# Gradient of four decode layers on one core: other positions for the last K and dK products of the last pass

## The chip, the cores and the metric

The kernel runs on one core of a Trainium2 chip. The metric is the device time of one execution in microseconds (us); less is better. The core's engines work side by side, each through its own instructions in order: PE (TensorE: matrix products and transposes), DVE (VectorE), ACT (ScalarE), POOL (GpSimd) and SP (SyncE). In this kernel SP issues the loads from memory (DMA queue q1), POOL the stores (q0), and ACT a few weight loads (q10); all of them are carried out by the same 16 DMA engines. PE writes to PSUM only, and DVE or ACT then copies ("evacuates") the result to on-chip memory.

## What is computed

Attention over a cache of 65,536 keys and a feed-forward layer, twice each with the same weights, for one token; and, for a given gradient of the result, the gradients with respect to the input, the caches, the weights and the biases. Cut to what matters:

```python
def A_ref(x, k_cache, v_cache, wq, wo):       # 32 query heads, 4 key/value groups, 128 wide
    q = (x @ wq) ...
    p = softmax(q @ K^T * Dh**-0.5)
    return (p @ V) @ wo
x = x + A_ref(layernorm(x), A_k_cache, A_v_cache, A_wq, A_wo)
x = x + B_ref(layernorm(x), ...)              # relu(h)^2 feed-forward
x = x + A_ref(layernorm(x), A_k_cache, A_v_cache, A_wq, A_wo)
x = x + B_ref(layernorm(x), ...)
# out_0 = x; out_1.. = vjp(grad_out): d x, d k_cache (out_2), d v_cache (out_3), d wq (out_4), d wo, ...
```

K and V caches are 64 MB each, so each is read in all four passes, and their gradients (another 64 MB each) are written in the last.

## The kernel before

The kernel goes through the caches in four passes: forward of the first attention, forward of the second, backward of the second, and the **last pass** (`attn_bwd4`), which is the backward of the first attention and writes the K and V gradients of both layers. Only the last pass is touched by the change.

**Items and half-blocks.** The last pass has 256 *items* (`ITEMS[3]`), in four groups of 64; an item is 8 columns of 128 keys. Four items make a *half-block* of 1 MB (`J` = 32 columns), the unit that is loaded (`kv8`, line 361) and stored (line 1441). I number the half-blocks of the last group from the end: V5, V4, ... V0 and K5, K4, ... K0, so that K0 is loaded and used last.

**Stages and lags.** `pipeline` (line 846) runs in steps. For each stage, item k is handled in step k + lag + 16 (the 16 is `LEAD`; the V stages run ahead by up to 16 steps at the start of the pass, by none from item 64 on). In the order of a step the stages are: `vT` transposes an item of V (lag 0; L1354 on PE, evacuated at L164 or L161 to `kt`), `vS` computes dP from it (lag 2; L1391, then X at L1412), `eIn` and `eT` prepare the saved probabilities (L1363, L1369), `dV8` forms outer products for dV (lag 3; L1435, from `GG[1]`), `xT` transposes X (lag 6; L1369), `dK8` forms outer products for dK (lag `DK_LAG` = 7; L1435, from `GG[0]`), and `k8` multiplies X with an item of K (lag `B4_LAG` = 11; L1466, eight products per item, 32 per half-block). Each half-block gives 1 MB of dV or dK: four PSUM tiles `ps_gg` of 128 x 1024, each made by two products of L1435 and cast to bf16 by ACT (L161) or DVE (L164) before the store. `ps_gg` has two buffers, shared with the other outer products (L1513, which form the weight gradients) and with the small L1498 transposes that prepare their rows.

**The end.** When the last K product is there, `fold_dq` (L1198 to L1203) forms the last group's dq, and `on4` runs the last chain: L723 multiplies dq with transposed weights, the layernorm's backward follows, and `g_outer_last` forms the last part of the gradient of wq: three preparations at L1498 (two of them, `rowa`, partly need nothing of dq), eight tiles at L1513, four stores of 512 KB at L1534. Three functions are placed by their distance from the end of the pipeline (`end`): `last_v`, which issues the loads of V2, V1 and V0 together; the weight loads `wq4` on ACT (L459); and `fill4`, which begins the transposes at L689. With a largest lag of 11 the pipeline has 283 steps and these stand in steps 260, 263 and 273.

**Where loads go.** On-chip memory has 20 slots of 1 MB (`ARENA`). In the last pass stores (`fill`) keep to one set of slots and loads to another, of seven slots. A load takes the slot that has been free longest in the program's order, and on the chip it waits until that slot's last user is done: for a slot that held K, the last L1466 product of that half-block; for one that held V, the last L1354 transpose. SP issues its loads in order, so one that waits holds up those behind it.

**Order.** Outside of `manual_schedule` blocks the order of each engine's instructions is made by a scheduler when the program is built; a step in `pipeline` decides what an instruction's place is in the program, not exactly where it comes out. The last pass is outside such blocks.

Of the kernel before, what the change touches and what calls it, by code (L numbers as in the profile page):

```python
# [20 lines left out]
def kernel(  # L21
# [44 lines left out]
    TLEAD = 2  # L66
# [213 lines left out]
    def hold(i):  # L280
        HELD.add(i)
        FREE.pop(i, None)
# [124 lines left out]
    DK_LAG = TLEAD + J // 8 + 1  # L407
    B4_LAG = DK_LAG + J // 8
    DV_LAG = TLEAD + 1
# [433 lines left out]
    def tasks(i):  # L843
        for fn in TASKS.pop(i, ()):
            fn()

    def pipeline(items, stages, bg, end=(), holds=(), lead=None):

        def due(lag):
            at = {}  # L850
            for k, it in enumerate(items):
                at.setdefault(k + lag + LEAD if lead is None or lag >= 0 else k + ~lag + lead(k), []).append(it)
            return at
        LEAD = 0 if lead is None else lead(len(items))
        when = [due(l) for _, l in stages]
        maxlag = max(l for _, l in stages) + LEAD
        for i in range(len(items) + maxlag):
            NOW["i"] = i
            NOW["wide"] = NOW["pairs"]
            for at, k in holds:  # L860
                if i == at:
                    hold(k)
            tasks(i - 0.5)
            for n, (fn, lag) in enumerate(stages):
                for it in when[n].get(i, ()):
                    fn(*it)
                if n == 0:
                    tasks(i)
            bg.step(max(0, i - LEAD))
            NOW["wide"] = False  # L870
            NOW["step"] += 1
            for before, fn in end:
                if i == len(items) + maxlag - before:
                    fn()
        while TASKS:
            k = min(TASKS)
            NOW["i"] = int(k + 0.5)
            tasks(k)
# [128 lines left out]
    def attn_fwd(p, L, on_group, bg, end=()):  # L1007
# [178 lines left out]
        with tc.manual_schedule(engines=ORDERED):  # L1186
            pipeline(items, [(kT, 0), (kS, TLEAD), (v8, FWD_LAG)], bg, end, holds)
# [19 lines left out]
    def attn_bwd3(p, L, on_group, bg, end=()):  # L1207
# [85 lines left out]
        with tc.manual_schedule(engines=ORDERED):  # L1293
            pipeline(items, [(vT, 0), (vS, TLEAD), (k8, B3_LAG)], bg, end)
# [3 lines left out]
    def attn_bwd4(p, La, Lb, on_group, bg, stack, end=()):  # L1298
        dspool = stack.enter_context(tc.tile_pool(name="b4_ds", bufs=2))
        items = ITEMS[p]  # L1300
# [181 lines left out]
        for b in range(V_LEAD * 8 // J // 2):  # L1482
            nexts.append(("k",) + items[(b + 2) * J // 8])
            nexts.append(("v",) + items[(b + NKEEP[2]) * J // 8])
        pipeline(items, [(vT, ~0), (vS, ~TLEAD), (eIn, 0), (eT, TLEAD), (dV8, DV_LAG), (xT, DK_LAG - 1), (dK8, DK_LAG), (k8, B4_LAG)], bg,
                 end, lead=V_SHIFT)


# [148 lines left out]
    bg = Background()  # L1637
# [39 lines left out]
    bg = Background()  # L1677
# [165 lines left out]
    bg = Background()  # L1843
# [130 lines left out]
    bg = Background()  # L1974
# [42 lines left out]
    def fill4():  # L2017
# [5 lines left out]
                                  lastg[3] * 1024)  # L2023
        next(PRE["gwq"])
    attn_bwd4(3, L1, L3, on4, bg, b4, [(12 + B4_LAG, last_v), (20, pre_load("wq4", lambda: wq_slabs(lastg[3], 2))), (10, fill4)])
    b4.close()
    ps4_stack.close()
# [30 lines left out]
```

## Time and profile before

| | us |
|---|---|
| three runs | 1932.66, 1934.70, 1939.24 |
| their median | 1934.70 |
| the profiled execution's own time | 1936.54 |
| its span, first to last instruction | 1934.7 |
| PE busy (matmul) | 1595.9 (82%) |
| DVE busy / ACT busy | 1171.8 (61%) / 1044.5 (54%) |
| mean rate of the DMA engines | 407 GB/s |
| last K product (L1466) starts | at 1900.30 |
| last evacuation ends, last store issued | 1928.1, 1928.36 |

The busy shares are means over four passes with different limits. What matters here is the stretch from about 1846 us to the end: what PE, the loads and the two `ps_gg` buffers do there. A row of the timeline gives the start, the busy time, the engine, the line, the operation with what it writes and reads, how many instructions of it stand together, and in brackets the engine's idle time before it with what ended it. A row of the windows gives, for a stretch of time, the busy time and number of instructions of each engine, the TensorE clock that was granted (1.00 is full), the share of the DMA engines' time and their rate.

### The profile page before, as it was taken

What the parts mean: (1) busy time and instruction counts of PE and PEld (TensorE: products, weight loads), DVE (VectorE), ACT (ScalarE), POOL (GpSimd) and SP (SyncE); (2) the same over time, 40 slices, a digit from 0 to 9 for tenths busy, and PEclk for the clock granted to TensorE, in tenths of its full rate; (3) what the DMA queues carried; (4) which work ended last, traced back from release to release, by engine and by line L of the source; (5) the groups of instructions that cost most, each with busy time, mean ns of one, the idle gap of its engine ahead of it and who ended that gap; (6) DMA issues with size and microseconds to landing.
All of it is one profiled execution on the core that took longest, in us unless ns stands there. A gap on an engine that the chain in (4) does not pass through costs nothing. (4 is left out here: it accounts for less than half of the span.)

```text
span 1934.7 us, 66770 instructions
## 1 busy us (share of the span) xinstructions
PE 1595.9 (82%) x30099; PEld 1303.7 (67%) x30099; DVE 1171.8 (61%) x2448; ACT 1044.5 (54%) x1619; POOL 143.4 (7%) x325
## 2 busy tenths in 40 slices
PE   6878788688778878978787888888978979789796
PEld 6878778678777778877777885555555555456463
DVE  5655555255555554645454576777867777667685
ACT  3434333345333545445363465666867677667676
POOL 0000000000000000000000002111211111111111
PEclk9989998799999998999899999898988889788896
DMA  9999999999999999999999997999999999999997
GB/s 394 426 428 424 427 429 416 403 420 415 428 425 428 429 414 327 376 426 429 425 426 422 404 366 285 425 424 386 424 425 423 424 402 407 393 403 416 421 419 301
DMA packets 107148, 787.62 MB, mean 407 GB/s; under 512 B 9440, under 2 KB 16622, under 8 KB 42222
## 3 DMA queue, kind: packets, MB, share of 16 engines
q1 hardware_dynamic: 78558, 609.26, 76.2%
q0 software_dynamic: 24080, 165.70, 20.5%
q10 hardware_dynamic: 4224, 8.39, 1.1%
q8 instruction: 235, 3.85, 0.7%
q14 instruction: 51, 0.42, 0.1%
HBM read 617.62 MB, written 165.69 MB: 405 GB/s over the span
## 5 line engine op out<-in xcount | busy, mean ns | idle before, releaser
L164 DVE COPY kt<-ps_tr 128x1024 bf16<-128x1024 bf16 x736 | 504.9, 688 | 434.6 <-PE ps_tr L1031 240.3
L161 ACT CAST arena<-ps_gg 128x1024 bf16<-128x1024 f32 x457 | 444.4, 1012 | 204.1 <-PE ps_gg L1435 136.3
L1031 PE MATMUL ps_tr<-ident_b,arena 128*128 128x128 bf16 x3840 | 312.4, 227 | 49.7 <-DMA arena<-in_A_k_cache_dram 37.0
L161 ACT COPY kt<-ps_tr 128x1024 bf16<-128x1024 bf16 x180 | 188.3, 1051 | 190.7 <-PE ps_tr L1225 108.9
L164 DVE CAST arena<-ps_gg 128x1024 bf16<-128x1024 f32 (+2 forms) x186 | 222.1, 1194 | 88.5 <-PE ps_gg L1435 51.1
L1031 PEld LDWEIGHTS <-arena 128*128 128x128 bf16 x3840 | 235.3, 102 | 58.6 <-DMA arena<-in_A_k_cache_dram 39.6
L1132 PE MATMUL ps_acc<-arena 128*128 128x64 bf16 (+4 forms) x4096 | 204.2, 196 | 46.4 <-DMA arena<-in_A_v_cache_dram 29.4
L1435 PE MATMUL ps_gg<-GG,xt 64*128 64x512 bf16 x1024 | 216.8, 420 | 19.5 <-ACT arena L161 8.8
L1354 PE MATMUL ps_tr<-ident_b,arena 128*128 128x128 bf16 x1824 | 181.2, 235 | 30.3 <-DMA arena<-in_A_v_cache_dram 16.4
L1049 PE MATMUL ps_sc<-L_qpad,kt 128*128 128x64 bf16 (+7 forms) x3584 | 183.5, 194 | 17.9 <-issue 10.9
L1114 ACT ACTIVATE arena<-S_sb,L_negm 128x128 bf16<-128x128 f32 x256 | 165.1, 1005 | 60.3 <-DVE L_negm L1099 60.3
L1225 PE MATMUL ps_tr<-ident_b,arena 128*128 128x128 bf16 x2032 | 161.7, 224 | 40.7 <-DMA arena<-in_A_v_cache_dram 39.0
L1132 PEld LDWEIGHTS <-arena 128*128 128x128 bf16 x4096 | 159.4, 101 | 52.4 <-DMA arena<-in_A_v_cache_dram 33.0
L1354 PEld LDWEIGHTS <-arena 128*128 128x128 bf16 x1824 | 120.7, 105 | 88.4 <-issue 68.7
L1049 PEld LDWEIGHTS <-kt 128*128 128x128 bf16 x3584 | 153.3, 100 | 21.8 <-issue 11.7
L1225 PEld LDWEIGHTS <-arena 128*128 128x128 bf16 x2032 | 122.6, 100 | 46.8 <-DMA arena<-in_A_v_cache_dram 41.3
L1466 PEld LDWEIGHTS <-arena 128*128 128x128 bf16 x2048 | 91.1, 101 | 63.1 <-DMA arena<-in_A_k_cache_dram 32.2
L1114 ACT ACTIVATION_READ_ACCUMULATOR arena<-S_sb,L_negm 128x1 f32 x256 | 128.0, 500 | 0.0
L1391 PEld LDWEIGHTS <-kt 128*128 128x128 bf16 x1824 | 85.2, 102 | 50.3 <-issue 48.7
L1391 PE MATMUL ps_sc<-DOB,kt 128*128 128x64 bf16 (+3 forms) x1824 | 118.2, 198 | 0.1
L1466 PE MATMUL ps_acc<-X,arena 128*128 128x64 bf16 (+3 forms) x1536 | 94.8, 197 | 26.3 <-DMA arena<-in_A_k_cache_dram 26.3
L585 ACT ACTIVATE mv_t<-mv_t 128x1024 bf16<-128x1024 bf16 x96 | 102.0, 1064 | 21.6 <-DVE mv_t L596 21.5
(319 smaller groups left out, 2102.8 us busy)
## 6 DMA issues: line engine op xcount, KB each, us to landing
arena<-in_A_k_cache_dram SPq DMA_DIRECT2D x82, 2048.0 KB, 21.4
arena<-in_A_v_cache_dram SPq DMA_DIRECT2D x79, 2048.0 KB, 20.7
out_dram<-arena POOLq DMA_DIRECT2D x149, 1024.0 KB, 15.2
arena<-in_A_v_cache_dram SPq DMA_DIRECT2D x84, 1024.0 KB, 12.6
arena<-in_A_k_cache_dram SPq DMA_DIRECT2D x84, 1024.0 KB, 12.8
arena<-in_A_wo_dram SPq DMA_DIRECT2D x22, 1024.0 KB, 13.9
arena<-in_B_w_dram SPq DMA_DIRECT2D x21, 1024.0 KB, 10.0
arena<-in_A_wq_dram SPq DMA_DIRECT2D x7, 2048.0 KB, 25.4
```

The lines of the kernel that those rows point to most:

```text
L161: nc.scalar.copy(out=out, in_=in_)
L164: nc.vector.tensor_copy(out=out, in_=in_)
L585: nc.scalar.activation(out=t[:, :], in_=t[:, :], func=ACTF.Copy, accum_out=y[:, kc:kc + 1])
L1031: nc.tensor.transpose(pt[:, i, :], kb8[:, i, :], ident_b[:, :])
L1049: nc.tensor.matmul(state["ps_s"][:, s:s + w, :].rearrange("p a b -> p (a b)"), lhsT=kt[:, i, :], rhs=L["qpad"][:, g, 0:w, :].rearrange("p ...
L1114: nc.scalar.activation(out=E(p, g, c0, SU)[:, :, h], in_=S[:, h, :], func=ACTF.Exp, bias=L["negm"][:, g, su, h:h + 1], scale=SCALE, accum_ ...
L1132: nc.tensor.matmul(ps_o[:, 0:w, :], lhsT=vb8[:, i, :], rhs=E(p, g, c, w), start=(c % SU == 0), stop=(c % SU == SU - 1), skip_group_check=True)
L1225: nc.tensor.transpose(pt[:, i, :], vb8[:, i, :], ident_b[:, :])
L1354: nc.tensor.transpose(pt[:, i, :], vb8[:, i, :], ident_b[:, :])
L1391: nc.tensor.matmul(state["ps_dp"][:, s:s + w, :].rearrange("p a b -> p (a b)"), lhsT=vt[:, i, :], rhs=DOB[:, g, 0:w, :].rearrange("p a b - ...
L1435: nc.tensor.matmul(pg[:, 512 * h:512 * h + 512], lhsT=xt[64 * h:64 * h + 64, j1 // 8 + m, :], rhs=gg[64 * h:64 * h + 64, :, :].rearrange(" ...
L1466: nc.tensor.matmul(ps_dq[:, 0:w, :].rearrange("p a b -> p (a b)"), lhsT=kb8[:, i, :], rhs=X[:, s:s + w, :].rearrange("p a b -> p (a b)"), ...
```

## The change

It lets the lag of a stage be a function of the item, and gives two stages such a function at the end of the pass.

- `k8`: the last 16 items (half-blocks K3 to K0) get a smaller lag. It is 11 for the sixteenth item from the end, then 10, 10, 10 for K3; 9, 9, 9, 8 for K2; 8, 8, 7, 7 for K1; 7, 6, 5, 5 for K0. The last K product moves from step 282 to step 276.
- `dK8`: the items of the second last half-block get lag 11 in place of 7, those of the last get 9. Their dK outer products move from steps 273 and 274 to 277 and 278 (second last) and from 277 and 278 to 279 and 280 (last).
- `maxlag`, from which the number of steps follows, is now 25 in place of 27, so the pipeline has 281 steps, and the three functions placed from its end move by two steps: `last_v` from 260 to 258, `wq4` from 263 to 261, `fill4` from 273 to 271.

```diff
         def due(lag):
             at = {}
+            if callable(lag):
+                for k, it in enumerate(items):
+                    at.setdefault(k + lag(k) + LEAD, []).append(it)
+                return at
             for k, it in enumerate(items):
                 at.setdefault(k + lag + LEAD if lead is None or lag >= 0 else k + ~lag + lead(k), []).append(it)
             return at
         LEAD = 0 if lead is None else lead(len(items))
         when = [due(l) for _, l in stages]
-        maxlag = max(l for _, l in stages) + LEAD
+        maxlag = max(l(len(items) - 1) if callable(l) else l for _, l in stages) + LEAD
...
-        pipeline(items, [(vT, ~0), (vS, ~TLEAD), (eIn, 0), (eT, TLEAD), (dV8, DV_LAG), (xT, DK_LAG - 1), (dK8, DK_LAG), (k8, B4_LAG)], bg,
+
+        def k_lag(k):
+            left = len(items) - 1 - k
+            return B4_LAG - min(5, (max(0, 15 - left) + 2) // 3) - (left < 2)
+
+        def dK_lag(k):
+            left = len(items) - 1 - k
+            return DK_LAG + (0 if left >= 8 else 4 if left >= 4 else 2)
+        pipeline(items, [(vT, ~0), (vS, ~TLEAD), (eIn, 0), (eT, TLEAD), (dV8, DV_LAG), (xT, DK_LAG - 1), (dK8, dK_lag), (k8, k_lag)], bg,
                  end, lead=V_SHIFT)
```

## The prediction

> **What bounds the kernel now.** First the page's slices, then stretches of the last 90 us, then the timeline where the change begins.
>
> ```profile
> span 1934.7 us, 66770 instructions
> ...
> PEclk9989998799999998999899999898988889788896
> DMA  9999999999999999999999997999999999999997
> ```
>
> DMA is full up to the last slice, the clock is not.
>
> ```profile
> 1846.00:1856.00 10.00, 9.40 (x136) 5.89 (x133) 8.13 (x19) 7.78 (x9) 2.31 (x4) 1.00 1.01 422
> ...
> 1886.00:1896.00 10.00, 9.60 (x124) 6.41 (x123) 8.29 (x13) 8.51 (x10) 1.06 (x2) 1.00 1.02 422
> ...
> 1904.00:1914.00 10.00, 8.92 (x86) 4.86 (x83) 5.28 (x16) 5.54 (x8) 1.25 (x2) 0.50 0.58 239
> 1914.00:1924.00 10.00, 6.56 (x29) 1.56 (x28) 5.88 (x7) 5.55 (x6) 2.34 (x4) 0.50 0.63 262
> ```
>
> In the first two rows PE is busy 94 and 96% at full clock, more than DVE (81 and 83%) and ACT (78 and 85%): the rows say that PE's own queue sets the pace, and what PE loses there comes late at the end. From 1904 on nothing is full: there the two `ps_gg` buffers go round (fill, cast, fill), at half clock.
>
> Where the last K product stands, and how the loads before it are timed:
>
> ```profile
> 1845.57 0.37 PE L1466 MATMUL ps_acc<-X,arena 128*128 128x64 bf16 x8
> ...
> 1845.97 0.33 SPq L361 DMA_DIRECT2D arena<-in_A_v_cache_dram  x1
> ...
> arena<-in_A_v_cache_dram SPq DMA_DIRECT2D x1, 1024.0 KB, 9.1
> ...
> 1855.92 0.31 PE L1466 MATMUL ps_acc<-X,arena 128*128 128x64 bf16 x6
> ...
> 1900.30 0.18 PE L1466 MATMUL ps_acc<-X,arena 128*128 128x16 bf16 x1
> ```
>
> K7's last products start at 1845.57 and free a slot; V0's load goes out 0.2 us after their end, and lands 9.1 us later, at 1855.1. K6's last six start at 1855.92, K0's last at 1900.30.
>
> **The change, part by part.** *K's smaller lags.* Nothing is added or removed; products move in PE's queue. The order of the built program shows how far: K3's last product comes 33 products earlier, K2's 68, K1's 12, and K0's, the one that the last chain needs, 2 products later than before. The scheduler has put other work in front of it. In the stretch before, 139 products (K7's end to K6's) took 10.3 us, 13.5 a us, so the last K product gains nothing: +0.1 us.
>
> *`last_v` two steps sooner.* The loads of V2, V1, V0 now stand in front of K5's on SP and take the slots that K5, V2 and V1 had (of V6, K8 and V5). K5 gets the slot that V0 had, K7's. Its load before went out at 1825.72, now when V0's did, at 1845.97, behind V0, as V0 was behind V1: it lands at 1855.1. The first weight load (`wq4`) is now seven instructions earlier on ACT and takes V4's slot, free at about 1847; it shares the DMA engines with K5's load. That costs K5's load between 0 and 3.1 us (with weight loads under way, the load of 1865.66, one ahead of it, took 12.2 us against these 9.1). I take 0.5, near the lower end, as K5's is under way first: 1855.6.
>
> When does PE need K5? Its order now has K5's first two products right behind K6's, and everything else of PE behind them. Of the 139 products between K7's end and K6's, 32 have moved behind: ten of L1435, four of L1513, eight of L1498, nine of L1386 and L1391, one of L1336. By start-to-start times of the timeline (a pair of L1435 0.33, of L1513 0.34, eight of L1498 0.33, the rest 0.6) that is 1.65 + 0.68 + 0.33 + 0.6 = 3.3 us. K6 ended at 1856.1, so now at 1852.8. PE then waits 1855.6 - 1852.8 = **2.8 us**. Ends: 0, if PE comes there late; 5.4, with the dearer weight load. Behind the waiting product stand all of PE's transposes and outer products, so DVE, ACT and the stores run dry as well; before, K5 was there from 1838.7 on (its load took 13.0 us) and nothing waited.
>
> *What a wait of that size does to the clock* stands in the same pass:
>
> ```profile
> 1533.29 0.41 PE L1513 MATMUL ps_gg<-rowb,rowa 2*128 2x512 bf16 x2 [2.94 <-ACT arena L161]
> ...
> 1760.84 0.23 PE L1354 MATMUL ps_tr<-ident_b,arena 128*128 128x128 bf16 x1 [2.22 <-DMA arena<-in_A_v_cache_dram]
> ```
>
> ```profile
> 1533.50:1543.50 10.00, 10.00 (x86) 5.35 (x84) 5.68 (x10) 6.03 (x6) 1.06 (x2) 0.52 1.01 424
> ...
> 1762.00:1775.70 13.70, 13.70 (x133) 8.19 (x132) 9.78 (x16) 9.88 (x13) 1.62 (x3) 0.52 1.02 419
> ...
> 1776.00:1786.00 10.00, 9.58 (x129) 6.20 (x126) 8.40 (x14) 9.85 (x15) 2.76 (x5) 0.98 1.02 427
> ```
>
> After idle gaps of 2.94 and 2.22 us PE ran at about half clock for 10 to 13.7 us. There it did 133 products, which at the full clock behind it (129 in 10.0) take 10.3 us: a loss of **3.4 us**. Ends: 0 (no drop) and 3.7 (113 products in 13.2 us after the gap at 1714, against 119 in the 10 us behind). I take 3.4.
>
> The Trainium skill ("TensorE: Matmul & The Clock Gate", Part 1) has the clock fall to half after at least one idle window of about 3.4 us, and asks for no gap over about 3 us. By that rule 2.8 us could pass, and the sum would be without the 3.4, about 1937.6; the two rows above, 2.22 and 2.94 us, speak against it, and I go by them.
>
> *K4, K1, K0.* K4's load waits for V3's transposes; its first product comes 118 products behind them, 8.7 us at full pace, and by the same ratio of 13.7 to 10.3 some 11.6 at half clock. K1's load alone took 9.2 us. So the slow clock hides it: 0; with a full clock it would cost 0 to 1.6 (load of 1860.71: 10.3). K1's load waits for K3's end, 134 products or 9.9 us ahead of its use; K0's for V0's transposes, 178 or 13.2 us: 0 each. `fill4` brings the L689 transposes forward by two steps, before the last K product in both kernels: 0.
>
> *dK behind the last K product.* Fills of `ps_gg` behind that product: before 26 (11 of L1435, 12 of L1513, 3 of L1498), ending at 1928.1, so 27.8 / 26 = 1.07 us each; now 25. The dK tiles of the last two blocks were behind it before, too; what moves is that the eight of wq now go first and the eight of dK last. So -1.07. On POOL the last store is now 1 MB in place of 512 KB; stores of 1 MB issued at 1915.95 took 4.1 us, the last one of 512 KB 3.0: +1.1. Nothing waits behind it but the program's end. Together 0. Ends: a fill takes 0.70 us where PE keeps the full clock (0.33 + 1.01 + gaps, two buffers), 25 x (0.70 - 1.07) = -9; and +1.1 without the saved fill.
>
> **The sum.** 0.1 + 2.8 + 3.4 + 0 + 0 = +6.3 us. The profiled execution took 1936.5 (span 1934.7 and 1.8 around it), 1.8 above the median of the runs; with the change 1942.8, and as a median **1941.0**.
>
> **Rivals.**
> A, *faster*: the end is set by the last chain and the fills. For it: 30 of the last 34 us are neither full DMA nor full PE, and the gradient of wq no longer stands behind the dK tiles. Against it: the count of fills falls only by one. If K5's load is in time, and the tail keeps PE's clock half of the way, a fill costs 0.88: 25 x 0.88 = 22.0 in place of 27.8, then +1.1: 1934.7 - 4.7 = 1930.0; at full clock throughout, 25 x 0.70 + 1.1 gives 1925.5. Middle 1928. It decides where K5 lands before 1853 and no gap over about 2 us stands behind 1900.
> B, *it changes nothing*: PE comes to K5 about when it lands, because casts hold it up. For it: PE's order has fewer outer products there but the same casts of `kt`. Then 1934.7 + 0.1 = 1934.8.
> C, *two waits*: the clock stays full or recovers before K4, K4's load (1.6) or K1's (9.9 against up to 10.3, 0.4) stops PE too and a second drop follows: 1941.0 + 1.6 + 3.4 = 1946. For it: K5 is in front of K4 on SP, so whatever delays the one delays the other; against it, the slow clock gives K4 time.
>
> **How the numbers follow.** My forecast 0.50, between 1937 and 1945; A 0.17; B 0.15; C 0.18. A measurement of this kernel tells about 0.3% (5.8 us) from no change. Slower by more than that is above 1940.5: C and 0.29 of my forecast, 0.47. Within it: 0.21 of the forecast and B, 0.36. Faster: A, whose middle lies beyond 1928.9: 0.17. The range 1928 to 1948 leaves out half of A and the dearest of C.
>
> **What would show it.** After: K5's load issued near 1846, in front of a gap of 2 to 4 us on PE at an L1466 with K's load as its releaser, between 1852 and 1857; a granted clock near 0.5 in the 10 us behind it; K0's last product near 1906.5; then eight fills of wq and eight of dK, some 34 us from there to the end. It is wrong if no such gap is there, if the clock stays at 1.00 behind it, or if the time from the last K product to the end is other than 33 to 36 us.

## The result, and the profile after

The changed kernel took 1947.63 us (median of 7 runs, 1942.19 to 1953.91), the kernel before 1934.07 (7 runs on the same chips, 1931.54 to 1941.48): a ratio of 1.0066, with a 95% interval of [1.0041, 1.0091]. So it is 13.6 us slower by the medians, 12.8 by the ratio, 8 to 18 by the interval; 6.3 were forecast, with a median of 1941.0 and a range of the forecast of 1937 to 1945. The execution profiled below took 1952.2 us.

The page's slices of the changed kernel: the TensorE clock and the DMA engines' share.

```profile
span 1950.0 us, 66773 instructions
...
PEclk9989998699998998998898999888988889879887
DMA  9999999999999999999999998999999999999997
```

A slice is 49 us wide, so nothing of the loss can be seen here. The clock's last three digits are 8, 8, 7, before 8, 9, 6: the tail ran at a somewhat higher clock, the stretch ahead of it at a lower one.

PE's timeline of the changed kernel at the two places that matter (start, busy time, line, operation; in brackets the idle time before it and what ended it). L1470 is the K product (L1466 before):

```profile
1856.61 0.37 PE L1470 MATMUL ps_acc<-X,arena 128*128 128x64 bf16 x8
1862.13 0.29 PE L1470 MATMUL ps_acc<-X,arena 128*128 128x64 bf16 x2 [5.16 <-DMA arena<-in_A_k_cache_dram]
...
1875.20 0.29 PE L1395 MATMUL ps_sc<-DOB,kt 128*128 128x64 bf16 x4
1877.63 0.41 PE L1470 MATMUL ps_acc<-X,arena 128*128 128x64 bf16 x8 [2.14 <-DMA arena<-in_A_k_cache_dram]
```

K6's last products end at 1856.97, and PE then stands 5.16 us for the load of K5. Only 13 us later it stands again, 2.14 us, for the load of K4. In the kernel before no gap over 1 us lies between K7's end and K0's last product.

The changed kernel's windows in steps of 10 us from K7's end (PE, PE's weight loads, DVE, ACT, POOL, granted clock, DMA share, rate in GB/s):

```profile
1851.13:1861.13 10.00, 5.59 (x107) 4.34 (x105) 5.93 (x15) 3.99 (x5) 1.82 (x3) 1.00 1.01 419
1861.13:1871.13 10.00, 9.00 (x111) 6.33 (x111) 5.11 (x13) 3.62 (x4) 1.10 (x2) 0.66 0.95 343
1871.13:1881.13 10.00, 7.79 (x93) 4.67 (x91) 6.25 (x9) 5.11 (x6) 1.15 (x2) 0.90 0.96 343
1881.13:1891.13 10.00, 9.86 (x110) 5.73 (x108) 6.17 (x15) 7.25 (x8) 2.42 (x4) 0.76 0.96 399
1891.13:1901.13 10.00, 9.69 (x145) 6.28 (x143) 7.73 (x15) 7.95 (x10) 1.80 (x3) 1.00 0.74 256
1901.13:1911.13 10.00, 9.45 (x129) 6.38 (x124) 8.34 (x17) 8.40 (x10) 1.06 (x2) 1.00 0.99 391
```

PE did 421 products in the first 40 us; the kernel before did 581 in the 40 us behind its K7 end (1845.94). Two of its windows, for comparison:

```profile
1855.94:1865.94 10.00, 9.23 (x167) 7.15 (x168) 8.43 (x16) 5.35 (x6) 2.23 (x4) 1.00 1.02 419
1865.94:1875.94 10.00, 9.74 (x138) 6.16 (x135) 7.92 (x18) 7.42 (x8) 1.89 (x3) 1.00 1.01 419
```

The last column says the same for the transfers: over these 60 us the rates add to 21.5 MB, in the kernel before (420, 419, 419, 420, 423, 399 GB/s) to 25.0 MB. The DMA engines did not simply stand idle: their busy share is still 0.95 and 0.96 where the rate is 343, and only in the fifth window, at 0.74, are they idle for a good part. There the loads wait for PE: K1's goes out at 1896.59, when K3's last product has ended, and K0's at 1900.50. 3.5 MB, or 8.3 us at 420 GB/s, have to be moved later.

The clock behind the two gaps:

```profile
1862.10:1868.90 6.80, 6.77 (x65) 4.43 (x66) 2.96 (x6) 3.62 (x4) 1.10 (x2) 0.50 0.93 329
1879.10:1885.90 6.80, 6.80 (x64) 3.86 (x63) 3.02 (x5) 4.96 (x5) 1.26 (x2) 0.50 0.97 387
```

Half clock, but only 6.8 us each time. At full clock e6 does 133 products in 10 us in this part of the pass (its second window below); so the 65 and 64 products were worth 4.9 and 4.8 us, and each stretch lost about 2 (1.8 by the prediction's measure, 129 products in 10 us).

The tail of the changed kernel, from the first fills that nothing but `ps_gg` holds up:

```profile
1933.50 0.62 PE L1525 MATMUL ps_gg<-rowb,rowa 2*128 2x512 bf16 x2 [0.27 <-ACT arena L161]
1934.55 1.28 PE L1439 MATMUL ps_gg<-GG,xt 64*128 64x512 bf16 x4 [0.43 <-DVE arena L164]
...
1940.33 1.04 PE L1439 MATMUL ps_gg<-GG,xt 64*128 64x512 bf16 x4 [0.89 <-DVE arena L164]
```

As the change says, the fills of wq (L1525, before L1513) go first and the dK tiles (L1439, before L1435) last.

The bookkeeping of one execution each. K7's end is a good point to start from: up to there all kernels shown here but two (e7 and e9) have the same instructions of PE in the same order, and differ only behind it.

| us | before | changed | |
|---|---|---|---|
| start to K7's end | 1845.9 | 1851.1 | +5.2 |
| K7's end to the end of K0's last product | 54.5 | 66.1 | +11.6 |
| start of K0's last product to the end of the program | 34.4 | 33.0 | -1.4 |
| K7's end to the end of the program | 88.7 | 98.9 | +10.2 |

The first row is not shown to be the change's work. K7's end lay between 1836 and 1851 us in the profiled executions of the ten kernels with the same PE instructions up to there. In seven of these ten, the changed kernel's among them, PE has a gap of 4.4 to 5.3 us at a transpose of V about 30 us ahead of K9, and in three, the kernel before's among them, it has not. But the loads of `last_v` do go out ahead of K7's end, so a part of that row cannot be excluded as theirs. Comparisons of single executions are therefore made from K7's end on; I call that stretch the *end stretch*. The two gaps (7.3 us) and the two half-clock stretches (about 3.9) together are some 11.2 of the 11.6 us of the second row.

### The profile page after: what moved, and what is told of

Its sections match the earlier page's. It is cut to its first block, busy times and chain, and to the rows that moved or that the text cites. A ratio compares the mean times of both kernels' runs of the same rounds, so it can differ in the third digit from the quotient of the medians.

```text
span 1950.0 us, 66773 instructions
## 1 busy us (share of the span) xinstructions
PE 1607.4 (82%) x30099; PEld 1311.0 (67%) x30099; DVE 1173.6 (60%) x2448; ACT 1044.4 (54%) x1619; POOL 143.3 (7%) x325
## 5 line engine op out<-in xcount | busy, mean ns | idle before, releaser
L1035 PE MATMUL ps_tr<-ident_b,arena 128*128 128x128 bf16 x3840 | 311.8, 227 | 44.3 <-DMA arena<-in_A_k_cache_dram 32.6
L1439 PE MATMUL ps_gg<-GG,xt 64*128 64x512 bf16 x1024 | 218.3, 422 | 15.1 <-ACT arena L161 4.3
L1053 PE MATMUL ps_sc<-L_qpad,kt 128*128 128x64 bf16 (+7 forms) x3584 | 184.1, 194 | 20.6 <-issue 10.9
L1053 PEld LDWEIGHTS <-kt 128*128 128x128 bf16 x3584 | 153.1, 100 | 25.3 <-issue 12.9
L1470 PEld LDWEIGHTS <-arena 128*128 128x128 bf16 x2048 | 92.2, 102 | 71.3 <-DMA arena<-in_A_k_cache_dram 37.7
L1470 PE MATMUL ps_acc<-X,arena 128*128 128x64 bf16 (+3 forms) x1536 | 96.6, 199 | 31.6 <-DMA arena<-in_A_k_cache_dram 31.6
## 6 DMA issues: line engine op xcount, KB each, us to landing
arena<-in_A_v_cache_dram SPq DMA_DIRECT2D x84, 1024.0 KB, 12.8
```

The lines of the kernel that those rows point to most:

```text
L1035: nc.tensor.transpose(pt[:, i, :], kb8[:, i, :], ident_b[:, :])
L1053: nc.tensor.matmul(state["ps_s"][:, s:s + w, :].rearrange("p a b -> p (a b)"), lhsT=kt[:, i, :], rhs=L["qpad"][:, g, 0:w, :].rearrange("p ...
L1439: nc.tensor.matmul(pg[:, 512 * h:512 * h + 512], lhsT=xt[64 * h:64 * h + 64, j1 // 8 + m, :], rhs=gg[64 * h:64 * h + 64, :, :].rearrange(" ...
L1470: nc.tensor.matmul(ps_dq[:, 0:w, :].rearrange("p a b -> p (a b)"), lhsT=kb8[:, i, :], rhs=X[:, s:s + w, :].rearrange("p a b -> p (a b)"), ...
```

## The experiments

The question is which of the edits made the loads of K5 and K4 late. Three things moved by two steps because the pipeline became shorter (`last_v`, `wq4`, `fill4`); the lags of K and dK are the other two edits. The theory ("late loads"): the gaps are loads whose slot comes free too close to their use. Rivals: the new order of PE's work itself costs the time, or `last_v` alone does. Each kernel is the kernel before or the changed one with the edit shown. Results first:

| kernel | K7's end to K0's end, us | tail, us | end stretch, us | gaps of PE over 1 us for a load | ratio to before, 95% interval |
|---|---|---|---|---|---|
| before | 54.5 | 34.4 | 88.7 | none | |
| changed | 66.1 | 33.0 | 98.9 | K5 5.16, K4 2.14 | 1.0066 [1.0041, 1.0091] |
| e1 | 60.2 | 33.6 | 93.6 | K4 2.93 | 1.0022 [1.0004, 1.0039] |
| e2 | 54.5 | 31.8 | 86.1 | none | 1.0020 [1.0002, 1.0037] |
| e3 | 57.7 | 37.0 | 94.5 | K0 1.90 | 1.0027 [1.0010, 1.0045] |
| e4 | 54.9 | 32.1 | 86.8 | none | 0.9987 [0.9967, 1.0006] |
| e5 | 55.3 | 32.7 | 87.8 | none | 1.0000 [0.9982, 1.0019] |
| e6 | 55.6 | 32.6 | 88.0 | none | 1.0003 [0.9987, 1.0020] |
| e7 | 61.2 | 32.4 | 93.4 | K3 1.85, K1 1.08 | 0.9978 [0.9964, 0.9992] |
| e8 | 63.2 | 34.1 | 97.1 | K4 2.16, K1 2.10 | 1.0037 [1.0016, 1.0057] |
| e9 | 66.4 | 30.5 | 96.6 | K3 2.08 | 0.9978 [0.9964, 0.9991] |
| e10 | 55.6 | 32.7 | 88.1 | none | 1.0015 [0.9997, 1.0032] |

The ratios come from 12 runs each, beside 35 runs of the kernel before for e1 to e4 (median 1936.8 us) and 29 for the others (1934.3 us). Waits for a load of 0.3 to 0.6 us are left out of the table: one at K4 in e3 (0.27) and one at K1 in each of e5, e6 and e10 (0.34, 0.57, 0.60).

### Undoing the three moves

**e1: the changed kernel, `last_v` back in its old step.**

```diff
-    ... [(12 + B4_LAG, last_v), (20, pre_load("wq4", ...)), (10, fill4)])
+    ... [(10 + B4_LAG, last_v), (20, pre_load("wq4", ...)), (10, fill4)])
```

> The changed kernel with one thing undone: last_v is back in step 260, so the loads of V2, V1 and V0 stand behind K5's again (K5 in V6's slot); wq4 and fill4 stay two steps sooner, both new lags stay. Theory 'late loads' (PE stops at K5's first product because K5's load waits for K7's slot): the 5.16 us gap of PE at K5 is gone and with it the first stretch at half clock, so from K7's end to K0's last product about 66.1 - 5.2 - 1.7 = 59 us; the gap at K4 (2.14 us) may stay, as K4 still takes V3's slot, with its half clock. Time some 6 to 9 us under the changed kernel, about 1939 to 1942. Rival 'order' (the new lags themselves, which put other work in front of K0, cost the time): K7's end to K0's last product stays at 64 to 66 us and the time within 2 us of the changed kernel. Rival 'clock by chance' (the half clock of a single execution): no gap moved, times as the changed kernel's.

K5's load has V6's slot again, the gap at K5 is gone, and the gap at K4 is left:

```profile
1857.59 0.29 PE L1395 MATMUL ps_sc<-DOB,kt 128*128 128x64 bf16 x4
1860.81 0.61 PE L1470 MATMUL ps_acc<-X,arena 128*128 128x64 bf16 x8 [2.93 <-DMA arena<-in_A_k_cache_dram]
```

The end stretch is 5.3 us shorter than the changed kernel's, the size of the gap that went. Behind K7's end PE's order here is, product by product, the changed kernel's, so the difference is that of the loads. So the place of `last_v` is needed for the gap at K5, and it has no part in the one at K4.

**e2: the kernel before, `last_v` alone two steps sooner.**

```diff
-    ... [(12 + B4_LAG, last_v), (20, pre_load("wq4", ...)), (10, fill4)])
+    ... [(14 + B4_LAG, last_v), (20, pre_load("wq4", ...)), (10, fill4)])
```

> The kernel before with one thing of the change: last_v two steps sooner (258), all lags as before; K5's load waits for K7's end, but PE's order is as before, where K5's first product stands 148 products behind K7's end (108 in the changed kernel). Theory 'late loads': what decides is load time (9.1 to 10.9 us) against the work in between; 148 products took 10.5 us, so a gap of 0 to 0.5 us at K5, no half clock, and the time of the kernel before within 2 us (1933 to 1937). Rival 'last_v alone' (the order of loads is the whole loss): 8 us and more over before, 1942 or above. Rival 'order': as before, 1934.

K5's load is as late as in the changed kernel, behind V2, V1, V0 and in K7's slot, and yet there is no gap, and K7's end to K0's end takes 54.5 us as before. The reason stands in the built program: here K5's first product is the 148th behind K7's last, as in the kernel before, in the changed kernel the 108th. So `last_v` alone is not enough. The median is 0.2% over the kernel before all the same, though the end stretch is none the longer for it; that remainder comes back below.

**e3: the changed kernel, all three back.**

```diff
-    ... [(12 + B4_LAG, last_v), (20, pre_load("wq4", ...)), (10, fill4)])
+    ... [(10 + B4_LAG, last_v), (18, pre_load("wq4", ...)), (8, fill4)])
```

> The changed kernel's two lag functions, with last_v, wq4 and fill4 back in steps 260, 263 and 273. In PE's order K6, K5 and K4 stand as before, K3 and K2 33 and 68 products sooner, K1 72 sooner, K0's last product where it was. Theory 'late loads': no gap of over 1 us behind 1846, K7's end to K0's last product 54 to 56 us, and behind it the tail of the changed kernel (33.0 in place of 34.4 us): 1931 to 1935. Rival 'order': the lags cost as in the changed kernel, 1943 or above.

The theory's expectation was missed: the gaps at K5 and K4 are gone, but another opened, at K0:

```profile
1882.45 0.18 PE L1470 MATMUL ps_acc<-X,arena 128*128 128x16 bf16 x1
1884.53 0.32 PE L1470 MATMUL ps_acc<-X,arena 128*128 128x64 bf16 x5 [1.90 <-DMA arena<-in_A_k_cache_dram]
```

K0's load went out at 1874.42 and landed at 1884.48, 1.9 us behind PE. It is the same mechanism at a place that I hadn't looked at: 118 products lie between V0's last transpose, which frees the slot, and K0's first product, in the changed kernel 178. The tail is 37.0 us here, the longest of all.

**e5: the changed kernel, `last_v` and `wq4` back, `fill4` left two steps sooner.**

```diff
-    ... [(12 + B4_LAG, last_v), (20, pre_load("wq4", ...)), (10, fill4)])
+    ... [(10 + B4_LAG, last_v), (18, pre_load("wq4", ...)), (10, fill4)])
```

> The changed kernel with last_v and wq4 back in steps 260 and 263; the new lags and fill4 two steps sooner stay. K5's load is in front of the V loads again and K4 has V4's slot, not V3's; in PE's order K6 to K4 stand as before, K0 as in the changed kernel. Theory 'late loads': no gap at K5 or K4 and no half clock between K7's end and K0's last product, 54 to 56 us; from K7's end to the program's end 86 to 89 us (before 88.7, changed 98.9, last_v alone put back 93.7). Rival 'order' (the lags, which put K products in front of their loads): a gap at K1 or K0 as in the run with all three functions back (1.90 us, tail 37.0), 92 to 95 us.

No gap over 1 us for a load, an end stretch of 87.8 us, a ratio of 1.0000. Against e3 only `fill4` differs, so the gap at K0 came with the two lags at `fill4`'s old step. With both lags in place and the loads of K5 and K4 where they were, the kernel is neither slower nor faster: the lags' order of PE costs nothing by itself. It is not all of the changed kernel's order, since K5's first product is the 148th behind K7's end here.

### Which of the moves does it

**e8: the kernel before, `wq4` alone two steps sooner.**

```diff
-    ... [(12 + B4_LAG, last_v), (20, pre_load("wq4", ...)), (10, fill4)])
+    ... [(12 + B4_LAG, last_v), (22, pre_load("wq4", ...)), (10, fill4)])
```

> The kernel before, with nothing changed but wq4 two steps sooner (step 261, as in the changed kernel). Two facts of the built program: K4's load now takes V3's slot (free later) in place of V4's, and PE's order has K5's first product 108 products behind K7's end in place of 148; K5's load keeps V6's slot, and is early. Theory 'late loads' (each gap is a load whose slot comes free too near to its use): no gap at K5; a gap of 2 to 3.5 us at K4 (2.14 in the changed kernel, 2.93 with last_v back), about half clock behind it for 7 to 14 us, and 92.5 to 95 us from K7's end to the program's end against 88.7 before; the ratio between 1.001 and 1.004. Rival 'last_v is all of it': without K5's late load nothing is lost: no gap over 1 us, 87 to 89 us, ratio 0.998 to 1.001.

The moved weight load alone costs 0.37%, more than half of what the whole change does. The gap at K4 is the size expected, and there is one more, at K1, which I had not expected and which took the end stretch to 97.1 us, over the expected 95:

```profile
1866.10 0.29 PE L1391 MATMUL ps_sc<-DOB,kt 128*128 128x64 bf16 x4
1868.55 0.41 PE L1466 MATMUL ps_acc<-X,arena 128*128 128x64 bf16 x8 [2.16 <-DMA arena<-in_A_k_cache_dram]
...
1898.22 0.35 PE L1466 MATMUL ps_acc<-X,arena 128*128 128x64 bf16 x7
1900.67 0.26 PE L1466 MATMUL ps_acc<-X,arena 128*128 128x64 bf16 x3 [2.10 <-DMA arena<-in_A_k_cache_dram]
```

Two things come with the weight load's new step. The load takes V4's slot, and K4's load, which had it, is left with V3's, which comes free later. And the scheduler builds another order: K5's first product is 108 products behind K7's end and K1's first 119 behind K3's end (129 before). It is this order, not K's new lags, that takes 40 products from in front of K5: it is there in e8 without the lags, and e5 and e10 have the lags with 148 products.

**e10: the changed kernel, `wq4` alone back.**

```diff
-    ... [(12 + B4_LAG, last_v), (20, pre_load("wq4", ...)), (10, fill4)])
+    ... [(12 + B4_LAG, last_v), (18, pre_load("wq4", ...)), (10, fill4)])
```

> The changed kernel with wq4 alone back by two steps (step 263, in the same step as K4's load, behind it). last_v stays two steps sooner, so K5's load still stands behind V2, V1, V0 and gets K7's slot; but PE's order has K5's first product 148 products behind K7's end again, and K4's load gets V4's slot. Theory 'late loads': K5's load lands 10 to 11.5 us behind K7's end, and 148 products take about 10.9 us there: a gap at K5 of 0 to 1 us, none at K4; 86.5 to 89 us from K7's end to the program's end, ratio 0.998 to 1.001. Rival 'last_v alone is enough': a gap of 3 us or more at K5 with half clock behind it, 92 to 96 us, ratio 1.002 to 1.005.

PE goes from K6's end to K5's first products without a stop:

```profile
1861.63 0.36 PE L1395 MATMUL ps_sc<-DOB,kt 128*128 128x64 bf16 x7
1861.83 0.37 PE L1470 MATMUL ps_acc<-X,arena 128*128 128x64 bf16 x7
1862.28 0.39 PE L1439 MATMUL ps_gg<-GG,xt 64*128 64x512 bf16 x2
```

One thing differs from what was expected: K5's load took 9.3 us (issued 1851.48, landed 1860.78), not 10 to 11.5. The first weight load goes out at 1861.78 here, behind it; in the changed kernel it goes out at 1852.41, beside it, and K5's load took 10.9. PE came 1.0 us after the landing (K6's last product ends at 1861.75). With `last_v` still two steps sooner, `wq4` alone makes both gaps go, and 10.8 us of end stretch with them. The ratio's interval takes in 1, though its middle is above what was expected.

**e6: the changed kernel, the loads of K5 and K4 put in front of V2, V1, V0.**

```diff
     def last_v():
+        for g, c8 in ITEMS[3][-6 * J // 8:-4 * J // 8:J // 8]:
+            kv8("k", g, c8)
         for g, c8 in ITEMS[3][-3 * J // 8::J // 8]:
```

> The changed kernel whole, but last_v, still in step 258, first issues the loads of K5 and K4 and then those of V2, V1 and V0: K5 gets V6's slot, K4 K8's, and the three V loads get those of V5, K7 and V4. Theory 'late loads': no gap at K5 and K4; the V loads have some 10 us to spare and make none; K7's end to the program's end 86 to 89 us, the time at or under that of the kernel before. Rival 'V then waits': a gap of 1 to 5 us moves to a V transpose, 92 us or more.

Every step of the change is kept, and the edit changes only the order in which slots are handed out: K5 takes V6's, K4 K8's. Both gaps go, and with them the loss (1.0003). But PE's order comes out other too: behind K7's end it is, product by product, that of e5 and e10, with K5's first the 148th. The weight load, though at its new step, gets K6's slot again (it goes out at 1851.62, K6 ends at 1851.58); in the changed kernel, e1 and e8 it has V4's (it goes out at 1852.41, 1842.34 and 1850.84, each within 0.05 us of the end of V4's last transpose). So the changed kernel's order goes with the slot that the weight load gets, not with its step alone, and it is e1 and e2, not e6, that keep the loads and the order apart. The windows of this kernel show PE at full clock and the transfers at 417 to 423 GB/s, where the changed kernel's fell to 343:

```profile
1856.00:1866.00 10.00, 9.76 (x146) 6.51 (x142) 8.12 (x14) 4.77 (x5) 1.82 (x3) 1.00 1.02 422
1866.00:1876.00 10.00, 9.61 (x133) 6.24 (x131) 7.42 (x16) 8.23 (x9) 1.70 (x3) 1.00 1.02 417
```

### What the change could give, and the older gap

**e4: the changed kernel with K's old lag; dK's new lag alone is left.** The largest lag is 11 again, so all three functions keep their steps.

```diff
-        ... (dK8, dK_lag), (k8, k_lag)], bg,
+        ... (dK8, dK_lag), (k8, B4_LAG)], bg,
```

> The kernel before with the dK part alone: the dK products of the last two blocks get lags 11 and 9, K keeps 11, the three functions keep their steps. No load moves. Theory 'late loads': no new gap; only the tail changes: 0 to -1.5 us, 1932 to 1935. Rival 'dK last' (eight dK tiles and a 1 MB store at the very end cost more than the tiles of wq did): the tail grows by 1 to 3 us over 34.4, 1935 to 1938.

The tail is 2.3 us shorter than before, the end stretch 1.9; the ratio's interval holds 1. dK's new place gains little, if anything.

**e7: e4, and `rowbw`'s slot taken from the stores' set.** In the kernel before PE stands 8.4 us at K9, from 1801.8, for a load whose slot `rowbw` had used:

```profile
1810.17 0.50 PE L1466 MATMUL ps_acc<-X,arena 128*128 128x64 bf16 x6 [8.37 <-DMA arena<-in_A_k_cache_dram]
```

```diff
-        rsl = Slot("rowbw")
+        rsl = Slot("rowbw", True)
```

> The dK part alone (lags 11 and 9 for the dK products of the last two blocks) and one slot moved: the rows for the gradient of w1 (rowbw) take a slot of the store set and not one of the load set. In every profile so far PE stops for 8.1 to 8.5 us some 45 us ahead of K7's end, for K9's load, which waits for the slot of those rows. Theory 'late loads' (a load that gets its slot less than about 11 us of PE's work ahead of its use stops PE, and the half clock comes on top): that gap and the 10.2 to 13.7 us at half clock behind it are gone, 8 + 2.5 us, and the tail is that of the dK part, 32 us: 8 to 12 us under the kernel before, 1925 to 1928 against 1936.8. Rival 'DMA-bound stretch' (the DMA engines are full there anyway, and a gap filled in one place opens in another): no more than 3 us.

That gap went, but 8 to 12 us were not gained: it is 0.22%, 4.2 us by the ratio, a little over the 3 of the rival. Two new gaps stand in the last group, the second of them here:

```profile
1884.83 0.18 PE L1470 MATMUL ps_acc<-X,arena 128*128 128x16 bf16 x1
1886.09 0.35 PE L1470 MATMUL ps_acc<-X,arena 128*128 128x64 bf16 x5 [1.08 <-DMA arena<-in_A_k_cache_dram]
```

**e9: e6 and `rowbw`'s slot together.**

```diff
-        rsl = Slot("rowbw")
+        rsl = Slot("rowbw", True)
```

> The changed kernel with the loads of K5 and K4 ahead of last_v's (as in e6_k_first, which left no gap at K5 or K4) and the slot of rowbw taken from the stores' set (as in e7_dk_rowbw, which took K9's gap of 8.4 us away). Theory 'the gaps add': K9's gap goes, nothing over 1 us comes in its place, 87 to 89 us from K7's end, and the whole gains what K9's gap and its half clock cost: 8 to 12 us, ratio 0.993 to 0.997. Rival 'the loads' chain moves on' (as in e7): with PE 8 us further ahead, loads whose slots come free at a fixed place in PE's order (K3's at K5's end, K1's at K3's) are late in their turn: one or two gaps of 1 to 2 us with half clock, 92 to 95 us from K7's end, ratio 0.997 to 1.000.

The rival held in kind, with gaps a little over its 1 to 2 us and an end stretch of 96.6 us over its 92 to 95. K7 ended at 1829.5, 16 us sooner than before, and K0 only 4.6 us sooner: a gap of 2.23 us behind K6 (for `xin`, a copy on POOL, which had itself stood 4.35 us for a store to land), one of 2.08 at K3, each with half clock behind it. The windows of e9 from K7's end say where the lead went:

```profile
1829.48:1839.48 10.00, 8.96 (x125) 5.60 (x124) 8.24 (x20) 6.68 (x8) 1.26 (x2) 1.00 1.01 420
1839.48:1849.48 10.00, 7.69 (x91) 5.94 (x90) 4.96 (x10) 4.54 (x5) 2.85 (x5) 0.66 1.01 422
...
1859.48:1869.48 10.00, 7.92 (x84) 4.34 (x80) 4.13 (x8) 5.65 (x6) 1.15 (x2) 0.67 1.02 418
```

In these stretches the DMA engines are full (418 to 422 GB/s) although PE stands. From its K7 end to its last instruction e9 had 34 MB to move (rate by time, over all windows of the stretch), the kernel before 31.5: PE had run ahead of the transfers, and most of what it gained came back as waits. e7 and e9 are both shown faster than the kernel before (0.9978 each), the only ones here, by some 4 us.

### One row for every gap

From the landings in the traces, for each gap at a K product: when its load was issued and landed, and when PE came.

| gap | issued | landed | took | PE came | PE waited |
|---|---|---|---|---|---|
| changed, K5 | 1851.16 | 1862.08 | 10.9 | 1856.97 | 5.16 |
| changed, K4 | 1867.01 | 1877.59 | 10.6 | 1875.49 | 2.14 |
| e1, K4 | 1850.09 | 1860.77 | 10.7 | 1857.88 | 2.93 |
| e3, K0 | 1874.42 | 1884.48 | 10.1 | 1882.63 | 1.90 |
| e7, K3 | 1853.64 | 1864.48 | 10.8 | 1862.67 | 1.85 |
| e7, K1 | 1876.83 | 1886.04 | 9.2 | 1885.01 | 1.08 |
| e8, K4 | 1858.59 | 1868.50 | 9.9 | 1866.39 | 2.16 |
| e8, K1 | 1890.03 | 1900.62 | 10.6 | 1898.57 | 2.10 |
| e9, K3 | 1852.64 | 1863.43 | 10.8 | 1861.40 | 2.08 |

Each was issued within 0.1 us of its slot's last use, and took 9.2 to 10.9 us. At the prediction's 13.5 products a us, a load must find its slot free some 125 to 147 products ahead of its use (an estimate): K5 with 148 had no gap in e2 and e10, with 108 it had 5.16 us; K4 with 118 had 2.14, K1 with 119 had 2.10 in e8. The count is a rough measure, since PE's pace varies with the products: the 118 in front of K4 took 8.5 us in the changed kernel, but the 141 in front of K3, which waits for K5's slot, only 9.1 and 8.8 us in e7 and e9, and K3 was late there. The kernel before shows how near the edge it is: K1 has 129 there, and no gap only because its load took 9.2 us.

## Why the prediction was right in kind and too small

**The mechanism was the one named**: K5's load, late behind V2, V1 and V0 and in K7's slot, stops PE, and the clock falls. e1 takes that load's lateness away, e10 the short way to it, e6 both, and the gap goes each time. The size was not: 1947.63 lies above the forecast's own 1937 to 1945, and 0.4 us inside the whole range of 1928 to 1948.

**K5's wait, 2.8 us forecast, 5.16 measured.** Both ends of the subtraction were off, by its own terms. The load was to land 9.7 us behind K7's end; it landed 10.95 behind. The weight load beside it seems to cost about 1 us and not the 0.5 taken from the range 0 to 3.1: the first load behind K7's end took 10.4 to 10.9 us in the three kernels that have a weight load beside it (changed, e1, e8), and 9.1 to 10.5 in the seven that have not (the kernel before, e2 to e6, e10). PE was to come 6.9 us behind K7's end; it came 5.84 behind. 2.8 + 1.3 + 1.0 is the 5.1 found. That 32 products had moved behind K5's was read correctly off the built order, but not asked where from: it comes with the slot that the weight load gets from its new step (e8; in e6 it has the step without that slot, and the order is the old one).

**K4, 0 forecast, 2.14 us measured: the step that failed.** The prediction let the slow clock hide K4's load: 118 products would take 11.6 us at half clock, longer than the load. The half clock lasted only to 1868.9, 1.9 us into those 118 products; PE did them in 8.5 us, the 8.7 that the prediction had for full clock, and the load took 10.6. This is what rival C says ("the clock stays full or recovers before K4"), and its second drop came too. C's price, 1.6 + 3.4 us over the forecast, comes to 1946; 1947.6 were measured. That it came so near is in part luck: K5's wait was 2.4 us dearer than in its sum, and the two half-clock stretches together about 2.9 us cheaper. Its chance of 0.18 looks low: the prediction itself showed that stretches of half clock end, and yet let one cover all of the 118 products.

**The clock, 3.4 us forecast once, about 2 us measured twice.** The direction was right, the length was not. The Trainium skill ("TensorE: Matmul & The Clock Gate", Part 1) has the clock fall after an idle window of about 3.4 us. The 5.16 us gap is over that, the gap of 2.14 us is under it and was followed by 6.8 us at 0.50, as were both of e8's gaps. The windows of e8 behind them:

```profile
1870.40:1877.20 6.80, 6.80 (x65) 3.89 (x61) 3.17 (x6) 4.95 (x5) 1.25 (x2) 0.50 1.02 425
1901.10:1907.90 6.80, 6.80 (x56) 4.53 (x55) 2.98 (x4) 3.86 (x4) 0.53 (x1) 0.50 0.86 360
```

So the choice of this kernel's rows over the rule held.

**K's smaller lags gain nothing (+0.1 forecast).** Right, and they lose a little: with them and without a gap over 1 us K7's end to K0's end takes 55.3 and 55.6 us (e5, e6), without them 54.5.

**K1 and K0, 0 each.** Right in the changed kernel: no gap there. But the margin was thin, as K1 in e8 and K0 in e3 show.

**The tail, 0 forecast (one fill less, 1.07; a last store of 1 MB, 1.1), -1.4 measured.** From K0's last product to the last evacuation 25 fills took 25.3 us, 1.01 us each against 1.07, which is 2.5 us less in place of 1.07 less; from there to the end 7.6 us in place of 6.6, 1.0 more in place of 1.1. The whole 33.0 us lies at the edge of the 33 to 36 that were to be seen. The order at the end, wq first and dK last, came as forecast.

**K0's last product, near 1906.5 forecast, 1917.07 measured.** Of the 10.6 us, 5.2 were there at K7's end already and are not shown to be the change's; of the other 5.4, the two waits were 4.5 more than forecast (5.16 + 2.14 - 2.8) and the two half-clock stretches 0.5 more than the one (3.9 - 3.4).

**Rivals A and B.** A asked that K5 land in time and the tail be faster: with that so (e5, e6, e10) the ratios are 1.0000 to 1.0015, and A's 1928 is not reached. B's premise, that PE comes to K5 about when it lands, is what e2 and e10 show for 148 products, and it is not so for 108.

**What stays open.** The end stretch explains 10.2 us, the medians differ by 13.6; the interval (8 to 18) allows that. But e2 and e10, both with `last_v` sooner and without a gap over 1 us in the end stretch, have medians 0.20 and 0.15% above the kernel before. Whether an earlier `last_v` costs 3 us ahead of K7's end, or these are the gap of 4.4 to 5.3 us that comes in some executions and not in others, was not settled: one profile a kernel cannot tell. The scheduler's other order stands in the three kernels whose weight load gets V4's slot (changed, e1, e8) and in none of the seven where it gets K6's; why the scheduler then chooses it was not tried.

## What to carry to other kernels

An edit that changes how many steps a pipeline has moves everything that is placed from its end, and here these moves made the loss: with `last_v` and `wq4` back the edit's own lags cost nothing (e5). Putting all three back was no cure (e3, 0.27% slower), as the lags then met a late load at K0. So list what is anchored to the end, and whose buffer each moved load now gets. For every load, count the work between the last use of its buffer and its own first use, and hold it against the load's time under traffic (9 to 11 us for the loads that PE met late here, 12 to 17 for those issued about 1 us behind another load); a load with less than that is a gap, and one with a little more becomes one when anything else moves. Where the transfers are full, taking one such gap away brings PE to the next.

## What was unexpected of the hardware

- Short gaps could be enough to halve TensorE's clock: 2.14 us for 6.8 us (changed), 1.85 us for 10.2 and 1.08 us for 3.4 (e7). They were not always: behind a gap of 2.69 us at a transpose of V in e10 (it ends at 1764.99) and one of 2.00 us in e4 (1760.33) the clock stayed full. All the stretches of half clock between 1780 us and the tail last 3.4, 6.8, 10.2 or 13.7 us, multiples of 3.4, and a longer gap did not mean a longer stretch: behind 5.16 us it was 6.8, behind 2.22 us in the kernel before 13.7. In each trace the changes of the clock lie on a grid of 3.41 us (in the changed kernel at 1862.05, 1868.88, 1879.12 and 1885.95). The gap of 2.14 us lies almost whole between two points of it, 1875.70 and 1879.12, and the one of 2.69 us in e10 is cut by one into 1.52 and 1.17 us; that this decides was not tested.
- A 1 MB load that PE had to wait for behind K7's end took 9.2 to 10.9 us from issue to landing; K9's, ahead of it, took 17.6 in the changed kernel (issued 1798.24, landed 1815.81).
- The transfers did not catch up behind a gap: 30 to 40 us after K5's wait they were down to 256 GB/s, with the loads of K1 and K0 held until K3's last product (1896.55) and V0's last transpose (1900.47) freed their slots.
